# The tails' group: layer 1 by seven block products, PSUM tiles for each half of C, and last stores of two batches' rows each

## Chip, cores and metric

One core of a Trainium2 chip (trn2). The metric is device time in microseconds (us), the median of several executions; every execution also gives a span (from the first to the last instruction) and the clock that TensorE was granted. Some executions fall into a slower state, with a lower granted clock; times are compared between the others ("fast"), within the same rounds. By the rule of 2% a ratio within 2% of 1 counts as "same"; smaller differences are given with their interval.

## The reference

Eight batches of attention over a causal window of 64 positions, then a feed-forward block with layer norm and a residual:

```python
scores = q @ k.T / 8, masked to 0 <= i - j < 64;  attn = softmax(scores) @ v    # 8 heads, 576 positions, 64 wide
x = attn.transpose(0, 2, 1, 3).reshape(8, 576, 512)
xn = (x - mean) / sqrt(var + 1e-6) * g_ln
out = x + relu(xn @ w_ch1) @ w_ch2                                               # 512 -> 2048 -> 512
```

## The kernel before

It works in nine groups of 512 rows. Groups 0 to 7 hold the first 512 positions of one batch each; group 8, the tails' group, holds the last 64 positions of all eight batches: block kb (of four) has batch 2kb in partitions 0 to 63 and batch 2kb+1 in partitions 64 to 127. While TensorE does one group's feed-forward block, the other engines do the next group's attention, so in group 8 they have little to do.

Layer 1 is plain: 16 column blocks `hps`, each of four matmuls of 128x512. Layer 2 is a 2x2 block product done with seven products in place of eight; three banks A, B, C of PSUM (the memory in which TensorE accumulates) collect them, and VectorE adds each result to `xn` (the residual, which becomes the output) as soon as it stands:

```python
def product(n, p):                                   # p: which half (128 rows) of the product
    which, a, wv = {1: ("A", ...), 2: ("B", ...), 6: ("A", ...), 5: ("C", ...),
                    7: ("A", ...), 4: ("B", ...), 3: ("C", ...)}[n]       # cut
    ...
    for c in range(NHC // 2):                        # 8 matmuls of 128x256
        nc.tensor.matmul(out=bank[which][:, p, :], lhsT=a[:, c, 128*p:128*p+128], rhs=wv[:, c, :],
                         start=(first and p == 0 and c == 0), stop=(c == NHC//2 - 1), ...)

def stage(n, p):                                     # order of n: 1, 2, 6, 5, 7, 4, 3
    product(n, p)
    ...                                              # after the second half: post() adds a bank to xn
    elif n == 7: post("A", 2, 1); post("C", 2, 1); post("A", 2, 0)

def store_rest(k0, cols, eng):                       # the tails' rows of blocks k0 and k0+1
    xv = x_norm[(g, k0 // 2)]                        # [128 partitions, 2 blocks, 512]
    for r in range(2):                               # r: half of the partitions
        (eng or (nc.sync, nc.scalar)[r]).dma_start(
            out=out[2*k0+r : 2*k0+r+3 : 2, SM:S, cols].rearrange("k s d -> s k d"),   # [64 rows, 2 batches, cols]
            in_=xv[64*r : 64*r+64, :, cols])
```

The softmax here doesn't subtract the row's maximum and nothing guards it: scores larger than these inputs give would overflow.

## Time and profile before

| | kernel before |
|---|---|
| median (3 executions) | 313.59 us (313.27 to 313.82) |
| traced execution | 314.71 us, span 313.0 us, clock 0.999 |
| last group, layer 1 | 64 matmuls, 13.84 us |
| last group, layer 2 | 112 matmuls, 12.25 us |
| last matmul to the end of the span | 5.5 us |

```profile
SPq L838 <- DMA out_dram<-xn: 2.7, 1, 2.7
```

Look at the engines' sum first (TensorE is the bound), then at the wait for the last stores, 2.7 us. The chain of waits, the last instructions and the DMA shares of this kernel stand in the prediction.

### The profile page before, as it was taken

Reading aid. Unit: us, or ns where it says so; the run is one execution under the profiler, and the core shown is the slowest. Engines: PE = TensorE matmul, PEld = TensorE weight load, DVE = VectorE, ACT = ScalarE, POOL = GpSimd, SP = SyncE. Lnnn points to the kernel's source line nnn. Section 1 sums busy time; section 2 is a strip of 40 time slices with the busy share of each in tenths; the row PEclk is TensorE's granted clock in tenths of the full one; section 3 lists DMA queues with packets and bytes.
Section 4 is the critical chain, followed back from the end, with each engine's and each line's share of the span. In section 5 each row is a group of like instructions: output and inputs, shape, how many; then the busy total and the mean of one; then the engine's idle time right before and its main releaser. Section 6 shows DMA issues by size and latency. Waiting matters only on the chain.

```text
span 313.0 us, 7473 instructions
## 1 busy us (share of the span) xinstructions
PE 298.9 (95%) x3041; PEld 194.1 (62%) x3041; DVE 205.2 (66%) x385; ACT 153.4 (49%) x258; POOL 166.3 (53%) x251
## 2 busy tenths in 40 slices
PE   6988998899999999999999999999999999999992
PEld 4457544497554468646964686459646855784582
DVE  1689585855674996589666965896669636751642
ACT  1496633477416752776247526762475058306500
POOL 7578666454760798369814983698145506200000
PEclk9999999999999999999999999999999999999999
DMA  8999999998866996798179997993690393003013
GB/s 192 267 390 290 320 336 272 280 304 184 159 144 196 268 206 105 243 312 147 37 212 316 203 149 219 316 142 67 209 172 19 62 209 117 2 2 134 0 36 101
DMA packets 109892, 57.42 MB, mean 183 GB/s; under 512 B 79841, under 2 KB 100833, under 8 KB 109858
## 3 DMA queue, kind: packets, MB, share of 16 engines
q1 hardware_dynamic: 108944, 54.02, 69.1%
q0 software_dynamic: 768, 2.80, 3.7%
q8 instruction: 24, 0.39, 0.5%
q10 hardware_dynamic: 146, 0.13, 0.1%
q14 instruction: 10, 0.08, 0.1%
HBM read 38.80 MB, written 9.44 MB: 154 GB/s over the span
## 4 chain that ended last, share of the span: by engine, by line
PE 74%; DMA 10%; DVE 7%; SPq 4%; POOL 2%; ACT 1%; issue 1%; POOLq 0%; ACTq 0%
PE hps L392 30%; PE pA L464 11%; PE pC L464 7%; PE pB L464 7%; PE ch L404 6%; DMA w2s<-in_moe_w_ch_dram 4%; DMA qk<-in_k_dram 4%; PE xps L317 3%; PE sc L283 3%; PE hph L513 3%; PE tp L226 2%; SPq L141 2%; DVE sS L443 2%; DMA w1s<-in_moe_w_ch_dram 2%; SPq L89 1%; DVE pt L297 1%
## 5 line engine op out<-in xcount | busy, mean ns | idle before, releaser
L392 PE MATMUL hps<-zT,w1g 128*128 128x512 f16 x480 | 110.4, 379 | 0.0
L396 ACT ACTIVATE hrT<-hps 128x512 f16<-128x512 f32 x120 | 71.9, 599 | 50.7 <-PE hps L392 47.2
L392 PEld LDWEIGHTS <-w1g 128*128 128x128 f16 x480 | 44.6, 98 | 49.3 <-issue 1.0
L290 ACT ACTIVATE pt<-sc 128x512 f16<-128x512 f32 x72 | 39.0, 595 | 29.8 <-DVE xn L471 15.6
L464 PEld LDWEIGHTS <-sS 128*128 128x128 f16 x448 | 43.3, 98 | 5.1
L342 POOL TENSOR_SCALAR rsz<-mvg 128x1 f32<-128x1 f32 x28 | 10.7, 382 | 60.4 <-DVE mvg L328 59.8
L128 POOL CAST qk<-qk 128x1024 f16<-128x1024 f32 x32 | 35.1, 1112 | 13.4 <-DMA qk<-in_q_dram 6.9
L464 PEld LDWEIGHTS <-hrT 128*128 128x128 f16 x336 | 32.6, 98 | 5.2
L212 ACT COPY qkT<-tp 128x1024 f16<-128x1024 f16 x16 | 16.1, 1012 | 35.2 <-PE tp L226 26.1
L297 DVE TENSOR_TENSOR pt<-pt,mask 128x1024 f16<-128x1024 f16 x32 | 25.4, 800 | 11.9 <-ACT pt L290 11.9
L471 DVE TENSOR_TENSOR xn<-pA,xn 128x512 f32<-128x512 f32 x28 | 19.2, 686 | 21.1 <-PE pA L464 21.1
L443 DVE TENSOR_TENSOR sS<-hrT 128x512 f16<-128x512 f16 (+1 forms) x42 | 24.8, 591 | 10.2 <-ACT hrT L396 10.2
L464 PE MATMUL pA<-wT,sS 128*128 128x256 f16 x224 | 26.9, 273 | 0.0
L345 POOL TENSOR_SCALAR z<-xn,rsz 128x512 f16<-128x512 f32 x28 | 25.3, 902 | 2.9
L464 PE MATMUL pC<-w2s,sS 128*128 128x256 f16 x224 | 26.8, 273 | 0.0
L325 DVE BATCH_NORM_STATS2 stats<-xn 128x6 f32<-128x512 f32 x36 | 25.0, 695 | 1.2
L323 DVE TENSOR_TENSOR xn<-xps,rcp 128x512 f32<-128x512 f32 x36 | 24.9, 692 | 1.2
L513 PE MATMUL hph<-zT,w1g 128*128 128x256 f16 x192 | 23.2, 272 | 2.3 <-ACT zT L360 1.1
L320 DVE RECIPROCAL rcp<-xps 128x8 f32<-128x8 f32 x36 | 7.4, 205 | 26.8 <-PE xps L317 26.8
L404 PE MATMUL ch<-w2s,hrT 128*128 128x512 f16 x96 | 23.1, 380 | 0.0
L513 PEld LDWEIGHTS <-w1g 128*128 128x128 f16 x192 | 18.3, 98 | 5.1 <-issue 2.6
L317 PEld LDWEIGHTS <-pt 128*64 128x64 f16 x576 | 12.2, 110 | 14.4 <-issue 6.4
(85 smaller groups left out, 395.1 us busy)
## 6 DMA issues: line engine op xcount, KB each, us to landing
out_dram<-xn SPq DMA_DIRECT2D x34, 256.0 KB, 2.6
qk<-in_q_dram SPq DMA_DIRECT2D x16, 512.0 KB, 6.2
qk<-in_k_dram SPq DMA_DIRECT2D x16, 512.0 KB, 7.4
v<-in_v_dram SPq DMA_DIRECT2D x32, 256.0 KB, 6.5
w2s<-in_moe_w_ch_dram SPq DMA_DIRECT2D x12, 512.0 KB, 5.7
w1s<-in_moe_w_ch_dram SPq DMA_DIRECT2D x4, 512.0 KB, 6.7
tk<-in_k_dram SPq DMA_DIRECT2D x8, 256.0 KB, 4.7
tv<-in_v_dram SPq DMA_DIRECT2D x8, 256.0 KB, 5.3
```

Source lines behind the costliest of these rows:

```text
L128: nc.gpsimd.tensor_copy(out=dst[:, :].rearrange("p (a j) e d -> p a e j d", j=j), in_=t[:, :].rearrange("p (a e j d) -> p a e j d", e=2, j ...
L290: nc.scalar.activation(out=o, in_=i, func=AF.Exp, bias=0.0, scale=scale)
L297: nc.vector.tensor_tensor(out=ptv, in0=ptv, in1=mb, op=ALU.mult)
L323: nc.vector.tensor_tensor(out=xn, in0=xps[:, :, 0:D], in1=rcp_b, op=ALU.mult)
L325: nc.vector.bn_stats(out=stats, in_=xv)
L345: nc.gpsimd.tensor_scalar(out=z, in0=xv, scalar1=rs, scalar2=nm, op0=ALU.mult, op1=ALU.add)
L392: nc.tensor.matmul(out=hps, lhsT=w1g[:, kc, 128 * hc:128 * (hc + 1)], rhs=zT[g][:, kc, :], start=(kc == 0), stop=(kc == NKC - 1),)
L396: nc.scalar.activation(out=hrT[:, hc, :], in_=hps, func=AF.Relu, bias=0.0, scale=1.0)
L404: nc.tensor.matmul(out=ch[kb], lhsT=hrT[:, hc, 128 * kb:128 * (kb + 1)], rhs=w2s[:, hc, :], start=(hc == 0), stop=(hc == NHC - 1),)
L443: nc.vector.tensor_tensor(out=o, in0=x, in1=y, op=op)
L464: nc.tensor.matmul(out=bank[which][:, p, :], lhsT=a[:, c, 128 * p:128 * p + 128], rhs=wv[:, c, :], start=(first and p == 0 and c == 0), st ...
L513: nc.tensor.matmul(out=hps[:, e], lhsT=w1g[:, kc, 128 * hc:128 * (hc + 1)], rhs=zT[g][:, kc, 256 * half:256 * half + 256], start=(kc == 0) ...
```

## The change

Its intent: do layer 1 of the tails' group by seven block products as well, which needs 7/8 of TensorE's work; the sums it needs go to engines that idle there. And shorten the tail: two PSUM tiles for C, so that each half of the last product is added and stored on its own, stores of whole blocks (two batches' rows), all issued from SyncE but one. The core of the diff:

```diff
         def store_rest(k0, cols, eng):
             for r in range(2):
-                (eng or (nc.sync, nc.scalar)[r]).dma_start(
-                    out=out[2 * k0 + r:2 * k0 + r + 3:2, SM:S, cols].rearrange("k s d -> s k d"),
-                    in_=xv[64 * r:64 * r + 64, :, cols],
+                (nc.sync, eng)[r].dma_start(
+                    out=out[2 * (k0 + r):2 * (k0 + r) + 2, SM:S, cols],
+                    in_=xv[:, r, cols],
@@ product: C of the last group
+                    for r in range(2):
+                        bank[("C", r)] = ps_t.tile([128, 256], FP32, tag=f"t{r}", ...)
@@ stage
+            if last and n == 3:
+                post_c(0, p)
+                nc.sync.dma_start(out=out[2 * p:2 * p + 2, SM:S, 256:DM], in_=x_norm[(g, 0)][:, p, 256:DM])
+                return
             elif n == 7:
                 post("A", 2, 1)
-                post("C", 2, 1)
+                post_c(2, 0); post_c(2, 1)            # last group
                 post("A", 2, 0)
+                store_rest(2, slice(256, DM), nc.sync)
             elif n == 4:
-                    store_rest(2, slice(0, DM), nc.sync)
+                    store_rest(2, slice(0, 256), nc.gpsimd)
@@ new: layer 1 in four blocks d; A, B, C in PSUM
+        def l1_a(d):  product 1 -> A; ACT keeps A; product 2 -> B; DVE: B + kept, POOL: ReLU; product 5 -> C; ACT keeps C
+        def l1_b(d):  product 6 onto A; ACT keeps A; product 3 onto C; DVE: C + kept, ReLU
+        def l1_c(d):  product 7 onto A; DVE: A + kept C, ReLU
+        def l1_e(d):  product 4 onto A; ACT: ReLU
@@ last group's order
+                l1_b(0); for d in 1..3: l1_a(d); l1_c(d - 1); l1_b(d); l1_e(d - 1)
+                stage(1, 0); l1_c(3); stage(1, 1); l1_e(3); stage(2, ...); stage(5, ...); stage(6, ...)
+                for n in (7, 4, 3): ...
@@ group before: sums of W1 (4) and of z (4) on VectorE; l1_a(0) ahead of its product 3
```

(The four `l1_` functions are shortened to what they do.)

More of the change, by code (lines that the diff above doesn't have):

```diff
@@ L458, in product @@
             if p == 0 and n in (1, 2, 5):
-                if which == "C":
+                if which == "C" and last:
+                    for r in range(2):
+                        bank[("C", r)] = ps_t.tile([128, 256], FP32, tag=f"t{r}", name=f"pC{r}_{g}")
+                elif which == "C":
                     bank[which] = ps_t.tile([128, 2, 256], FP32, tag="t1", name=f"p{which}_{g}")
@@ L462, in product @@
                     bank[which] = ps_mm.tile([128, 2, 256], FP32, tag="mm", name=f"p{which}_{g}")
+            split_c = last and which == "C"
+            o = bank[(which, p)][:, :] if split_c else bank[which][:, p, :]
             for c in range(NHC // 2):
                 nc.tensor.matmul(
-                    out=bank[which][:, p, :], lhsT=a[:, c, 128 * p:128 * p + 128], rhs=wv[:, c, :],
-                    start=(first and p == 0 and c == 0), stop=(c == NHC // 2 - 1), skip_group_check=True,
+                    out=o, lhsT=a[:, c, 128 * p:128 * p + 128], rhs=wv[:, c, :],
+                    start=(first and (p == 0 or split_c) and c == 0), stop=(c == NHC // 2 - 1), skip_group_check=True,
                 )
@@ L471, in post, with post_c @@
             nc.vector.tensor_tensor(out=xv, in0=bank[which], in1=xv, op=ALU.add)
+        def post_c(kb0, r):
+            xv = x_norm[(g, kb0 // 2)][:, r, 256:512]
+            nc.vector.tensor_tensor(out=xv, in0=bank[("C", r)], in1=xv, op=ALU.add)
         last = g == NGRP - 1
@@ L476, in stage @@
             product(n, p)
+            if last and n == 3:
+                post_c(0, p)
+                nc.sync.dma_start(
+                    out=out[2 * p:2 * p + 2, SM:S, 256:DM],
+                    in_=x_norm[(g, 0)][:, p, 256:DM],
+                )
+                return
             if p == 0:
@@ L488, in stage @@
                 post("A", 2, 1)
-                post("C", 2, 1)
+                if last:
+                    post_c(2, 0)
+                    post_c(2, 1)
+                else:
+                    post("C", 2, 1)
                 post("A", 2, 0)
+                if last:
+                    store_rest(2, slice(256, DM), nc.sync)
             elif n == 4:
@@ L501, in stage @@
                 tbank["n"] = 0
-                if last:
-                    store_rest(0, slice(256, DM), None)
-                else:
-                    store(0)
-                    store(1)
+                store(0)
+                store(1)
         def l1_half(half, i):
@@ L533, in l2_two, with l1_product @@
                     add_out(kb)
+        lbank = {}
+        def l1_product(n, d):
+            w1v = w1g[:, :, :].rearrange("p (a k) (i e m) -> p a k i e m", a=2, e=2, m=128)
+            t1, t2, t3, t4 = (zS["sum"][:, m] for m in range(4))
+            z = zT[g]
+            which, a, b = {
+                1: ("A", w1v[:, 0, :, :, 0, :], z[:, 0:2, 0:256]),
+                2: ("B", w1v[:, 1, :, :, 0, :], z[:, 2:4, 0:256]),
+                5: ("C", w1S[1], t1),
+                6: ("A", w1S[2], t2),
+                3: ("C", w1S[4], z[:, 2:4, 256:512]),
+                7: ("A", w1S[3], t3),
+                4: ("A", w1v[:, 1, :, :, 1, :], t4),
+            }[n]
+            if n == 1:
+                pool, tag = (ps_mm, "mm") if d == 2 else (ps_s, "sc")
+                lbank[("A", d)] = pool.tile([128, 2, 256], FP32, tag=tag, name=f"lA_{d}")
+            elif n == 2:
+                lbank[("B", d)] = ps_t.tile([128, 2, 256], FP32, tag="t0", name=f"lB_{d}")
+            elif n == 5:
+                if d % 2:
+                    lbank[("C", d)] = ps_t.tile([128, 2, 256], FP32, tag="t1", name=f"lC_{d}")
+                else:
+                    lbank[("C", d)] = ps_x.tile([128, 4, 256], FP32, tag="xps", name=f"lC_{d}")[:, 0:2]
+            o = lbank[(which, d)]
+            for r in range(2):
+                for kc in range(2):
+                    nc.tensor.matmul(
+                        out=o[:, r, :], lhsT=a[:, kc, 2 * d + r, :], rhs=b[:, kc, :],
+                        start=(n in (1, 2, 5) and r == 0 and kc == 0), stop=(kc == 1), skip_group_check=True,
+                    )
@@ new lines, in l1_quad, with l1_part, l1_keep, l1_sum @@
+        def l1_quad(d, e, h):
+            return hv[:, 2 * d:2 * d + 2, e, 256 * h:256 * h + 256]
+        def l1_part(x, d):
+            return zS[x][:, d % 2, :].rearrange("p (r t) -> p r t", r=2)
+        def l1_keep(x, which, d):
+            nc.scalar.copy(out=l1_part(x, d), in_=lbank[(which, d)])
+        def l1_sum(o, which, x, d):
+            nc.vector.tensor_tensor(out=o, in0=lbank[(which, d)], in1=l1_part(x, d), op=ALU.add)
+            eng = nc.gpsimd if x == "s1" else nc.vector
+            eng.tensor_scalar(out=o, in0=o, scalar1=0.0, scalar2=None, op0=ALU.max)
@@ new lines, in l1_a, with l1_b, l1_c @@
+        def l1_a(d):
+            l1_product(1, d)
+            l1_keep("s1", "A", d)
+            l1_product(2, d)
+            l1_sum(l1_quad(d, 0, 0), "B", "s1", d)
+            l1_product(5, d)
+            l1_keep("s5", "C", d)
+        def l1_b(d):
+            l1_product(6, d)
+            l1_keep("u2", "A", d)
+            l1_product(3, d)
+            l1_sum(l1_quad(d, 0, 1), "C", "u2", d)
+        def l1_c(d):
+            l1_product(7, d)
+            l1_sum(l1_quad(d, 1, 1), "A", "s5", d)
@@ new lines, in l1_e, with plan @@
+        def l1_e(d):
+            l1_product(4, d)
+            nc.scalar.activation(out=l1_quad(d, 1, 0), in_=lbank[("A", d)], func=AF.Relu, bias=0.0, scale=1.0)
+        if last:
+            def plan():
+                yield
+                l1_b(0)
+                for d in range(1, 4):
+                    l1_a(d)
+                    l1_c(d - 1)
+                    l1_b(d)
+                    l1_e(d - 1)
+                s_sums(0, 4)
+                stage(1, 0)
+                l1_c(3)
+                s_sums(0, 4, 1)
+                s_sums(4, 8, 1)
+                stage(1, 1)
+                l1_e(3)
+                s_sums(0, 4, 2)
+                stage(2, 0)
+                s_sums(4, 8, 2)
+                stage(2, 1)
+                stage(5, 0)
+                s_sums(0, 4, 3)
+                stage(5, 1)
+                s_sums(4, 8, 3)
+                stage(6, 0)
+                stage(6, 1)
+                s_sums(0, 4, 4)
+                s_sums(4, 8, 4)
+                for n in (7, 4, 3):
+                    for p in range(2):
+                        stage(n, p)
+                yield
+            l1_a(0)
+            return plan(), s_sums
@@ L552, in mlp_units, with w1_sums, z_sums @@
         return units, s_sums
+    w1S = {}
+    def w1_sums(*which):
+        wv = w1g[:, :, :].rearrange("p (a k) (i e m) -> p a k i e m", a=2, e=2, m=128)
+        a11, a12, a21, a22 = (wv[:, b, :, :, a, :] for a, b in ((0, 0), (0, 1), (1, 0), (1, 1)))
+        for n in which:
+            w1S[n] = p_in.tile([128, NKC // 2, NHC // 2, 128], FP16, tag=f"qk32_{n % 2}", name=f"w1S{n}")
+            o = w1S[n][:, :, :, :]
+            x, y, op = {1: (a21, a22, ALU.add), 2: (w1S.get(1), a11, ALU.subtract),
+                        3: (a11, a21, ALU.subtract), 4: (a12, w1S.get(2), ALU.subtract)}[n]
+            nc.vector.tensor_tensor(out=o, in0=x, in1=y, op=op)
+    zS = {}
+    def z_sums(g, *which):
+        if not zS:
+            t = p_in.tile([128, 4, 512], FP32, tag="v32", name="zsums", bufs=1)
+            zS["s5"] = t[:, 2:4, :]
+            zS["s1"] = p_in.tile([128, 2, 512], FP32, tag="tk32", name="s1sums", bufs=1)
+            zS["u2"] = p_in.tile([128, 2, 512], FP32, tag="tv32", name="u2sums", bufs=1)
+            zS["sum"] = t[:, 0:2, :].rearrange("p a n -> p (a n)").bitcast(FP16).rearrange(
+                "p (n k t) -> p n k t", n=4, k=2)
+        b11, b12 = zT[g][:, 0:2, 0:256], zT[g][:, 0:2, 256:512]
+        b21, b22 = zT[g][:, 2:4, 0:256], zT[g][:, 2:4, 256:512]
+        t1, t2, t3, t4 = (zS["sum"][:, n] for n in range(4))
+        for n in which:
+            o, x, y = {1: (t1, b12, b11), 2: (t2, b22, t1), 3: (t3, b22, b12), 4: (t4, b21, t2)}[n]
+            nc.vector.tensor_tensor(out=o, in0=x, in1=y, op=ALU.subtract)
     def w2_sums(i, c0, c1):
@@ L662, with begin_last @@
     load_qk(2, 1)
+    def begin_last():
+        nonlocal rest
+        rest, _ = mlp_units(NGRP - 1)
+        next(rest)
+    rest = None
     TAILS = {3: [0], 5: [1], 7: [2, 3]}
     for g in range(NGRP):
+        if g == NGRP - 1:
+            for _ in rest:
+                pass
+            break
         units, s_sums = mlp_units(g, (8, 16)[g] if g < 2 else 0, g == 0, g > 1)
@@ L806 @@
             at(8, t_tail, TAILS[g][1], 1)
+        if g == NGRP - 2:
+            at(0, w1_sums, 1, 2)
+            at(3, w1_sums, 3)
+            at(21, w1_sums, 4)
+            at(24, z_sums, NGRP - 1, 1, 2)
+            at(25, z_sums, NGRP - 1, 3, 4)
+            at(27, begin_last)
         for i, u in enumerate(units):
```

## The prediction

> **What bounds the kernel now.** I read the page first (busy shares and its 40 slices), then the chain of waits from 281.2 us to the end, then the timeline of the last microseconds, then the DMA view. TensorE is busy for 95% of the span at full granted clock, so what counts is TensorE's own work plus whatever lies behind its last matmul. The change touches only the last group (the tails' rows of all eight batches) and, on VectorE alone, the group before it. The chain of waits of that stretch:
>
> ```profile
> 281.35 13.84 PE hps L392 x64
> 295.19 1.75 PE pA L464 x16
> 296.94 1.75 PE pB L464 x16
> 298.69 1.75 PE pA L464 x16
> 300.44 1.75 PE pC L464 x16
> 302.18 1.75 PE pA L464 x16
> 303.93 1.75 PE pB L464 x16
> 305.68 1.76 PE pC L464 x16
> 307.44 0.02 issue
> 307.46 0.69 DVE xn L471
> ```
>
> Columns: start, length, what. There is no gap: layer 1 is 64 matmuls of 512 columns at 13.84/64 = 0.216 us, layer 2 is seven products of 16 matmuls of 256 columns at 1.75/16 = 0.109 us. No wait costs anything here. After the last matmul comes one VectorE addition, then stores:
>
> ```profile
> 306.88 1.98 SPq L424 DMA_DIRECT2D out_dram<-xn  x3
> 307.04 0.38 PE L464 MATMUL pC<-w2s,sS 128*128 128x256 f16 x2
> 307.46 0.69 DVE L471 TENSOR_TENSOR xn<-pC,xn 128x512 f32<-128x512 f32 x1 [0.61 <-PE pC L464]
> 308.18 0.70 ACTq L424 DMA_DIRECT2D out_dram<-xn  x1
> ```
>
> The span ends at 313.0, so the tail behind the last matmul is 5.5 us. It is the DMA engines' throughput that fills it: stretches of the DMA's share (last two columns: mean share of 16 engines, GB/s):
>
> ```profile
> 282.50:284.30 1.80, 1.80 (x10) 0.82 (x9) 0.00 (x0) 1.29 (x3) 0.00 (x0) 1.00 1.03 385
> 300.80:302.10 1.30, 1.30 (x14) 1.17 (x13) 0.70 (x2) 0.00 (x0) 0.00 (x0) 1.00 0.89 191
> 308.40:311.40 3.00, 0.00 (x0) 0.00 (x0) 0.00 (x0) 0.00 (x0) 0.00 (x0) 1.00 0.93 241
> 311.50:313.00 1.50, 0.00 (x0) 0.00 (x0) 0.00 (x0) 0.00 (x0) 0.00 (x0) 0.76 0.00 0
> ```
>
> The four last stores (two of 256 KB, two of 128 KB) keep all 16 engines 93% busy from 308.4 to 311.4; 1.6 us later the program ends. Stores of 128 partitions (first line) ran at 385 GB/s, those of 64 partitions (second line) at 191.
>
> **What the Trainium skill says.** (1) "DMA: Bandwidth & Descriptors", section "Why a DMA increments its semaphore by 16 and not by 1": a DMA is split along the slowest dimension of both access patterns, over the largest number k of engines, at most 16, that divides both sizes; on the SyncE and ScalarE queues these are the lowest-numbered k. Its section "Rules for kernel authors" says that an outermost dimension below 16 confines the whole DMA to that many engines. Every large transfer of the kernel before has 64 or 128 outermost and the trace shows them on all engines, so no transfer of it contradicts or tests this. The trace also records the destination as written: the old tail stores are 64 rows outermost, 2 batches inside. (2) "TensorE: Matmul & The Clock Gate", section "Wait — 56ns, not 53.3ns?": N columns take N/2.4 GHz + 2.5 ns, 109 ns for 256 and 216 for 512. The trace has 109 and 216: smaller matmuls lose almost nothing. (3) "VectorE: DVE Perf Modes", section "The perf-mode tier table (the rule you actually need)": tensor_tensor runs at one element a cycle with PSUM or fp32 operands, at two for fp16 in SBUF. The trace agrees: 0.69 us for 512 fp32, 0.42 for 512 fp16, 0.69 for 1024 fp16.
>
> **Layer 1, TensorE.** The new form has 7 products x 4 blocks x 4 matmuls = 112 of 256 columns, 112 x 0.109 = 12.2 us in place of 13.84. Gain 1.6 us, all on the path, if nothing waits.
>
> **The added work beside it.** In the group before, VectorE gets four sums of W1 (2048 fp16 a partition; from 0.42 at 512 and 0.69 at 1024, an estimate of 1.22 us each) and four of z at 0.42: 6.6 us. They are put where VectorE is idle (2.6 us before the mask, 2.1 before a reciprocal, 2.5 before the post of product 7), so TensorE should not feel them. In layer 1, per block: ScalarE three copies and a ReLU, 4 x 0.60 = 2.4 us; VectorE three additions with PSUM and two ReLUs, 3 x 0.69 + 2 x about 0.3 = 2.7; POOL one ReLU, about 0.8. TensorE takes 28 x 0.109 = 3.06 a block. Each engine fits, but tightly, so latencies show:
> - An accumulator's reader starts 0.20 us after the matmul's slot ends (the last pC: 305.51 + 16 x 0.109 = 307.26, VectorE at 307.46); with 0.69 for the addition and an estimated 0.06 back to TensorE a turn-round is 0.95. Product 4 accumulates on what product 7 left, and only products 6 and 3 (8 x 0.109 = 0.87) lie between. Laid out in order, with VectorE still at the previous addition in two cases, it waits 0.1, 0.2, 0.2, 0.1.
> - Layer 2's second product needs the ReLU of the very last product 4: 0.2.
> - The order of layer 2 in this group becomes 1, 2, 5, 6, 7 where it was 1, 2, 6, 5, 7. The addition that reads bank A after product 6 now stands right in front of product 7, which accumulates on A; nothing covers its turn-round: 0.95.
>
> Sum 1.7, against 1.6 gained. So I expect the last matmul at about the old time, 307.4 us.
>
> **The end.** With two PSUM tiles the last addition is 128x256: 0.69 - 256/0.96 ns = 0.42 us, 0.27 less, so the last store can be issued at about 308.0 instead of 308.18. Four stores had been issued from 306.88 on, 768 KB; half of those bytes for rows 2 and 3 now go out after product 7, some 1.8 us earlier. If they ran on 16 engines the tail would be latency only: issue at 308.0, first packet 1.24 us later (the stores issued at 299.44 have theirs at 300.68), last about 0.5 later, 1.6 to the end: span 311.4, a gain of 1.6.
>
> But the new destination is two batches of 64 rows, outermost 2, against 128 partitions. By the rule above k is 2: each 128 KB store runs on engines 0 and 1 alone, 64 packets of 1 KB each. In the packet records such a packet takes 46 ns undisturbed (the commonest of 12,800) and packets of one engine do not overlap (2 KB in 84 ns is 24.4 GB/s, x16 = 390, what the first line shows). So 64 x 0.046 = 2.94 us a store, one behind the other on the same two engines:
> - two stores after product 2, issued 299.3: 300.5 to 306.4, hidden;
> - two after product 7 (columns 256 on), ready from 306.3: to 312.3;
> - one after product 4 (the other goes by GpSimd): to 315.2;
> - two after the halves of product 3: to 321.1.
>
> Plus 1.6 to the end: span 322.7, and with the 0.6 by which the untraced median exceeds the traced span (313.59 against 313.0): 323.3 us. If GpSimd's store falls on the same two engines, 2.9 more: 326.2.
>
> **Rivals.**
> A. *The stores spread over 16 engines after all* (the compiler reorders the destination, or splits it to match the 128 partitions). For: it is a natural way to write the store, and a tuner who times it would see the loss. Against: the trace shows the old destination's dimensions kept as written. Time: 313.6 + 0.1 - 1.6 = 312.1.
> B. *As A, and the turn-rounds cost nothing* (or the product order is no wait): 310.4, still within 2%.
> C. *As A, but VectorE becomes the bound*: about 21 us of its work now lies in 27 us, and one late addition shifts all behind it; the two-source additions with fp16 may also hold up POOL's ReLU, which layer 2 needs first. Against: 3.06 us a block hold 2.7. Time 313 to 315.
> D. *k is 2 but stores on different pairs of engines*: then each takes 2.9 us beside the others: 308.0 + 1.2 + 2.9 + 1.6 + 0.6 = 314.3. Against: the page says lowest-numbered.
>
> **Range and chances.** I give the confinement to two engines three chances in four; then the time is 321 to 326.5, as packets take 40 or 46 ns and as GpSimd's store shares the pair or not, over the limit of 319.9 in nearly all cases. The rest lies at 310.5 to 315, within 2% (the limit is 307.3; even B does not reach it). A range for 8 in 10 has to span both: 311.6 to 326.6. Point 323.3.
>
> **What would show it.** In the changed profile: (1) DMA share of about 0.12 (2/16) and some 45 GB/s over the last 10 us, long after the last matmul, with stores landing 6 us and more after issue; shares of 0.9 would be A. (2) Seven products of layer 1 at 0.44 us, TensorE's last matmul between 306.5 and 308.5. (3) A TensorE gap of about 0.9 us ahead of product 7 in layer 2, released by VectorE's addition. (4) Small waits ahead of product 4 in layer 1, released by VectorE. (5) The last addition at 0.42 us. (6) The group before unchanged, its TensorE without new gaps. I am wrong if stores land in 2 to 3 us: then the answer is about 312.

## More of the kernel before

The page's first part and its list of transfers (engine, operation, number, KB each, us from issue to landing), with SyncE's own wait at the very end (us in total, times, longest):

```profile
span 313.0 us, 7473 instructions
...
PE 298.9 (95%) x3041; PEld 194.1 (62%) x3041; DVE 205.2 (66%) x385; ACT 153.4 (49%) x258; POOL 166.3 (53%) x251
...
out_dram<-xn SPq DMA_DIRECT2D x34, 256.0 KB, 2.6
```

## The result and the profile after

| | before | after |
|---|---|---|
| median of the same rounds | 313.43 us | 326.59 us (325.90 to 328.23, 4 executions) |
| traced execution | 314.71 us, span 313.0 | 327.09 us, span 325.1 |
| VectorE starts the last addition | 307.46 | 307.19 |
| last packet of the stores ends | 311.5 | 323.5 |

The ratio of the two is 1.0432 (95% interval 1.0384 to 1.0480). Ratios here are the mean time of one kernel's fast executions over that of the other's of the same rounds, so not quite the ratio of the medians quoted.

The first part of the page after. TensorE is busy a little less than before and the span is 12 us longer, so the time is not in work:

```profile
span 325.1 us, 7628 instructions
...
PE 297.6 (92%) x3089; PEld 198.2 (61%) x3089; DVE 217.4 (67%) x411; ACT 153.2 (47%) x258; POOL 172.8 (53%) x256
```

The last instructions of the kernel after (start, length, engine, what; in brackets the engine's idle time before it and who ended it):

```profile
299.06 1.91 PE L469 MATMUL pA<-wT,sS 128*128 128x256 f16 x16
301.00 0.69 DVE L476 TENSOR_TENSOR xn<-pA,xn 128x512 f32<-128x512 f32 x1 [1.00 <-PE pA L469]
...
301.75 1.91 PE L469 MATMUL pA<-wT,sS 128*128 128x256 f16 x16 [0.78 <-DVE xn L476]
...
306.87 0.92 POOL L424 DMA_DIRECT2D out_dram<-xn  x1 [13.75 <-DVE xn L476]
307.19 0.42 DVE L480 TENSOR_TENSOR xn<-pC,xn 128x256 f32<-128x256 f32 x1 [0.29 <-PE pC L469]
307.21 8.62 SPq L488 DMA_DIRECT2D out_dram<-xn  x2
```

The first three lines are products 6 and 7 and the addition between them: the wait foretold. The last addition takes 0.42 in place of 0.69 us and starts 0.27 us earlier. At 307.6 all arithmetic is done, where the kernel before had 308.15; yet the program ends at 325.1. Stretches of the DMA of the kernel after (last two columns: mean share of 16 engines, GB/s), against 0.93 and 241 before:

```profile
301.00:303.50 2.50, 1.75 (x17) 1.56 (x17) 1.89 (x3) 0.00 (x0) 0.00 (x0) 1.00 0.13 40
...
309.40:312.50 3.10, 0.00 (x0) 0.00 (x0) 0.00 (x0) 0.00 (x0) 0.00 (x0) 0.55 0.19 50
312.50:316.40 3.90, 0.00 (x0) 0.00 (x0) 0.00 (x0) 0.00 (x0) 0.00 (x0) 0.50 0.13 48
316.40:323.50 7.10, 0.00 (x0) 0.00 (x0) 0.00 (x0) 0.00 (x0) 0.00 (x0) 0.50 0.13 47
323.50:325.10 1.60, 0.00 (x0) 0.00 (x0) 0.00 (x0) 0.00 (x0) 0.00 (x0) 0.50 0.00 0
```

A share of 0.13 is two engines of sixteen. The stores run on for 15.9 us after the last addition (307.61 to 323.51); the 0.19 in one stretch comes with 16-byte packets on GpSimd's queue. Three more views: GpSimd's store by its time to landing (9.9 us), SyncE's wait for the stores at the end, and the two last issues of SyncE, whose durations (min/median/max in ns) are thousands of ns where the issues of the kernel before's tail take 595 to 702:

```profile
out_dram<-xn POOLq DMA_DIRECT2D x1, 128.0 KB, 9.9
```
```profile
SPq L1007 <- DMA out_dram<-xn: 7.9, 2, 5.2
```
```profile
L488 SPq DMA_DIRECT2D out_dram<-xn x2: 3613/4260/4907, 307.2 to 310.9; - x2
```

The chain of waits is no help at this end: from 293.1 to 306.8 it has nothing but "issue", and it ends with GpSimd's wait (POOLq L1007), not with SyncE's last stores. Where the chain does that, go to the DMA's shares.

The trace's packet records give each store of SyncE's queue (128 packets of 1 KB, median 46 ns each), in order:

| store | first packet to last | length |
|---|---|---|
| after product 2, block 0 | 300.11 to 303.53 | 3.4 |
| after product 2, block 1 | 303.52 to 306.25 | 2.7 |
| after product 7, block 2 | 306.24 to 309.73 | 3.5 |
| after product 7, block 3 | 309.69 to 312.53 | 2.8 |
| after product 4, block 2 | 312.53 to 317.86 | 5.3 |
| product 3, first half | 317.82 to 320.58 | 2.8 |
| product 3, second half | 320.54 to 323.51 | 3.0 |

They stand one behind the other. The records carry no engine number; that it is two engines follows from the share and from 64 x 0.046 = 2.94 us a store. Completion also shows the number of engines: the seven stores end with 14 semaphore writes on SyncE's queue, two each; in the kernel before every tail store has 16. GpSimd's store (32 packets of 4 KB at 159 ns: 16 x 0.159 = 2.54 us on each of two engines) runs from 312.28 to 316.33, beside the fifth store, which takes 2.5 us more than its neighbours. The share stays at 0.13 while both are under way: both are on the same two engines.

### The profile page after: what moved, and what is told of

Same layout as the page of the kernel before. It is cut to its first block, busy times and chain, and to the rows that moved or that the text cites. A ratio compares the mean times of both kernels' runs of the same rounds, so it can differ in the third digit from the quotient of the medians.

```text
span 325.1 us, 7628 instructions
## 1 busy us (share of the span) xinstructions
PE 297.6 (92%) x3089; PEld 198.2 (61%) x3089; DVE 217.4 (67%) x411; ACT 153.2 (47%) x258; POOL 172.8 (53%) x256
## 4 chain that ended last, share of the span: by engine, by line
PE 62%; DMA 14%; DVE 5%; SPq 5%; issue 5%; POOL 3%; POOLq 0%; ACT 0%
PE hps L392 24%; PE pA L469 9%; PE pC L469 6%; PE pB L469 6%; PE ch L404 5%; DMA w2s<-in_moe_w_ch_dram 4%; DMA qk<-in_k_dram 4%; SPq L141 4%; PE xps L317 3%; PE sc L283 3%; DMA vB<-vA 3%; DMA w1s<-in_moe_w_ch_dram 2%; DVE sS L443 2%; PE tp L226 1%; PE lA L582 1%
## 5 line engine op out<-in xcount | busy, mean ns | idle before, releaser
L392 PE MATMUL hps<-zT,w1g 128*128 128x512 f16 x416 | 96.3, 380 | 0.0
L396 ACT ACTIVATE hrT<-hps 128x512 f16<-128x512 f32 x104 | 62.3, 599 | 38.6 <-PE hps L392 35.1
L392 PEld LDWEIGHTS <-w1g 128*128 128x128 f16 x416 | 38.3, 98 | 42.0 <-issue 0.9
L532 PEld LDWEIGHTS <-w1g 128*128 128x128 f16 x192 | 18.0, 98 | 5.8 <-issue 2.0
```

What stands on the lines that cost most here:

```text
L392: nc.tensor.matmul(out=hps, lhsT=w1g[:, kc, 128 * hc:128 * (hc + 1)], rhs=zT[g][:, kc, :], start=(kc == 0), stop=(kc == NKC - 1),)
L396: nc.scalar.activation(out=hrT[:, hc, :], in_=hps, func=AF.Relu, bias=0.0, scale=1.0)
L532: nc.tensor.matmul(out=hps[:, e], lhsT=w1g[:, kc, 128 * hc:128 * (hc + 1)], rhs=zT[g][:, kc, 256 * half:256 * half + 256], start=(kc == 0) ...
```

## The experiments

Theory P: a destination with 2 outermost confines a store to two DMA engines, and eight such stores stand in line. Rival Q: it is SyncE's one queue with nearly all stores in it. Rival L: layer 1 and the waits it brings are the loss. Eleven runs of nine kernels; all gave correct results. The rounds ran on different chips, and the kernel before differs by 0.9 us between them, so go by the ratios. By the rule of 2% e2 and e4 are slower and all others the same.

| run | what | median us (before, same rounds) | ratio, 95% interval |
|---|---|---|---|
| e1_rows64 | after, 64 rows outermost | 313.20 (314.59) | 0.997, 0.994 to 1.000 |
| e2_before_pairs | before, new destinations | 327.33 (314.59) | 1.0422, 1.0385 to 1.0459 |
| e3_l1_only | before, new layer 1 and order | 313.49 (314.59) | 0.9971, 0.9947 to 0.9995 |
| e4_pool16 | after, only GpSimd's store on 16 engines | 324.21 (314.59) | 1.0311, 1.0287 to 1.0334 |
| e8_one_pair | e1, only the last store in the new form | 316.43 (313.69) | 1.0086, 1.0052 to 1.0119 |
| e5_order | e1, order 1, 2, 5, 6, 3, 7, 4 | 311.58 (313.69) | 0.9943, 0.9911 to 0.9976 |
| e6_order_2q | e5, halves on two queues | 311.47 (313.69) | 0.9917, 0.9890 to 0.9943 |
| e7_rows64_2q | e1, halves on two queues | 312.76 (313.69) | 0.9966, 0.9941 to 0.9991 |
| f1_l1_again | e3 again | 313.48 (314.22) | 0.9984, 0.9949 to 1.0019 |
| f2_before_tail | before, only the tail's halves and stores | 313.05 (314.22) | 0.9967, 0.9934 to 0.9999 |
| f3_best_again | e6 again | 312.20 (314.22) | 0.9937, 0.9906 to 0.9968 |

**e1_rows64.** Undo one part of the change.

```diff
-                    out=out[2 * (k0 + r):2 * (k0 + r) + 2, SM:S, cols],
-                    in_=xv[:, r, cols],
+                    out=out[2 * k0 + r:2 * k0 + r + 3:2, SM:S, cols].rearrange("k s d -> s k d"),
+                    in_=xv[64 * r:64 * r + 64, :, cols],
@@ product 3
-                nc.sync.dma_start(out=out[2*p:2*p+2, SM:S, 256:DM], in_=x_norm[(g, 0)][:, p, 256:DM])
+                for b in range(2):
+                    (nc.sync, nc.scalar)[b].dma_start(
+                        out=out[2*p+b, SM:S, 256:DM], in_=x_norm[(g, 0)][64*b:64*b+64, p, 256:DM])
```

> The changed kernel, with only the destinations of the tails' stores turned back: 64 rows outermost, two batches inside (store_rest), and for the two halves of product 3 one store per batch of 64 rows (SyncE and ScalarE). Queues otherwise as in the change. Theory P (a destination with 2 outermost confines each store to two DMA engines): the stores spread over 16 engines again, the DMA share in the last 5 us is 0.5 to 0.9, stores land in 2 to 4 us, span 310.9, time 311.5 to 312.5, 1.5 to 2 us below the kernel before. Rival Q (it is the one SyncE queue that holds nearly all stores, not the engines): the queue is as long as before, so 320 us or more. Rival L (layer 1 and the waits it brings are the loss): 324 us or more, since none of that is touched.

The loss is gone, with as many stores on SyncE's queue. DMA stretches of this run:

```profile
299.00:300.20 1.20, 0.58 (x6) 0.38 (x4) 0.58 (x1) 0.00 (x0) 0.00 (x0) 1.00 0.85 181
305.10:309.10 4.00, 0.67 (x7) 0.35 (x4) 0.84 (x3) 0.00 (x0) 0.71 (x1) 1.00 0.80 195
309.10:310.70 1.60, 0.00 (x0) 0.00 (x0) 0.00 (x0) 0.00 (x0) 0.00 (x0) 0.52 0.00 0
```

Shares of 0.8 and a span of 310.7: Q and L fall. The time missed the band of 311.5 to 312.5 by 0.7 us, but so did the kernel before in these rounds (314.59 where 313.6 was assumed); the difference of 1.4 us is just under the foretold 1.5 to 2.

**e2_before_pairs.** One part alone: the kernel before with the new `out=` and `in_=` of `store_rest`, nothing else.

> The kernel before, with only the destinations of its six tail stores in the new form (two batches outermost, 128 partitions); its queues, its layer 1 and its order stay. Theory P: 64 packets of 1 KB on each of two engines take 64 x 0.046 = 2.94 us a store, of 2 KB 64 x 0.084 = 5.4 us; two short ones hide behind TensorE, two long and two short ones stand after 308.1: 308.1 + 16.7 + 1.6 = 326.4 us of span, about 327 us. Rival Q: the last store stays on ScalarE's queue and the issue count is the old one, so 313 to 314. Rival L: nothing of layer 1 is changed, 313.5.

327.33 against the 327 worked out from two packet times. The new form of the tails' stores alone makes the whole loss, without any of layer 1, and with the last store on ScalarE's queue. The edit changes the source too, from 64 to 128 partitions; no run parts the two, but the stores of whole groups read 128 partitions and ran on all engines (share 1.03, first of the prediction's DMA stretches), so a 128-partition source alone doesn't confine a store. ScalarE's packets lie within those of SyncE's (312.06 to 319.74 of 307.07 to 324.23), and the share stays at that of two engines, so another issuing engine gives no other pair:

```profile
312.00:320.00 8.00, 0.00 (x0) 0.00 (x0) 0.00 (x0) 0.00 (x0) 0.00 (x0) 0.50 0.13 50
```

**e3_l1_only and f1_l1_again.** The change with the old C bank, the old last addition and the old stores; twice, since the first one's traced execution (319.83 us, clock 0.988) is left out.

> The change's layer 1 by seven products and its order of layer 2, with the old bank for C (one tile, one addition at the end) and the old stores. Theory P: the net of gain and waits alone; in the changed kernel's trace the last matmul's slot ends at 306.99 against 307.26 before, so 0.2 to 0.4 us faster than before: 313.0 to 313.4. Rival L: 320 us or more. Rival Q: as theory P.

> The same kernel as e3_l1_only (layer 1 by seven products and its product order alone, old bank for C, old stores), again, because the traced execution of that run was in the slow state and its three timed ones gave only an interval of 0.2 to 1.7 us. By the slow trace the stretch from the last product 4 of the group before to the last matmul is 27.65 us against 27.83 in the kernel before: 0.2 us faster, ratio 0.998 to 1.000. If layer 1 is worth the 1.6 us that its matmuls save: 0.995.

Layer 1 by seven products is worth 0.2% (interval from -0.5 to +0.2%) in the second run and 0.3% in the first: a small gain or none. The chain of waits of f1 shows where the 1.6 us of saved matmuls went:

```profile
292.73 0.44 PE lA L569 x4
293.17 0.87 PE pA L466 x8
294.04 0.50 PE lA L569 x4
294.54 0.66 PE pB L466 x6
...
295.23 1.27 PE pB L466 x10
296.50 1.75 PE pC L466 x16
298.25 1.76 PE pA L466 x16
...
300.03 0.70 DVE xn L473
...
300.77 1.91 PE pA L466 x16
```

From product 6's end (300.01) to product 7's (302.68) pass 2.67 us in place of 1.75: 0.92 lost to the addition's turn-round. Product 2 takes 1.96 (0.21 lost, waiting for the last ReLU), product 4's four blocks some 0.05 to 0.08 each, 0.2 in all. Sum 1.4 of 1.6; the stretch from the group before's last product 4 to the last addition is 27.67 us against 27.85 before.

**e4_pool16.** Only GpSimd's store, as two of one batch each.

```diff
-                    store_rest(2, slice(0, 256), nc.gpsimd)
+                    nc.sync.dma_start(out=out[4:6, SM:S, 0:256], in_=x_norm[(g, 1)][:, 0, 0:256])
+                    for b in range(2):
+                        nc.gpsimd.dma_start(out=out[6+b, SM:S, 0:256], in_=x_norm[(g, 1)][64*b:64*b+64, 1, 0:256])
```

> The changed kernel, with only GpSimd's one store made into two stores of one batch each (64 rows outermost), still from GpSimd; the seven on SyncE stay in the new form. Theory P with GpSimd's store on the same two engines: in the changed trace the fifth store of SyncE takes 5.3 us where its neighbours take 2.8; with GpSimd's bytes on all 16 engines it takes 2.8 to 3.2, so 2 to 2.5 us faster than the change: 324.1 to 324.6. If GpSimd's store had run on a pair of its own (my prediction's point): within 0.4 us of the change, 326.2 to 327.0.

324.21, inside the first band. SyncE's fifth store now takes 3.0 us (311.87 to 314.85) in place of 5.3, and from the end of the last addition to the last packet it is 13.4 us in place of 15.9. So GpSimd's store did run on the same two engines and cost about 2.5 us (2.4 by the medians; 3.8 by the ratios, since the kernel before was 1.2 us slower in these rounds than in the change's own).

**e8_one_pair.** One dose: e1 with only the very last store in the new form.

> As e1_rows64 (64 rows outermost everywhere), but the very last store, the second half of product 3, alone in the change's form with two batches outermost: one dose of the suspected cost where the change has eight. Theory P: 64 packets on each of two engines, 2.94 us, in place of two stores of 0.4 to 0.8 us on 16 engines: span 2.2 to 2.7 us over e1_rows64, about 315.5 us if the kernel before takes 314.6 (ratio to before 1.002 to 1.006). If the cost needs a queue of such stores (rival Q), nothing: ratio 0.997.

3.6 us over e1 by the ratios (3.7 over e7 below, of the same rounds), more than foretold. In the traces the last packet ends 6.1 us after the last addition, in e1 2.9. Its DMA stretches:

```profile
308.00:311.00 3.00, 0.00 (x0) 0.00 (x0) 0.00 (x0) 0.00 (x0) 0.00 (x0) 1.00 0.64 151
311.00:314.00 3.00, 0.00 (x0) 0.00 (x0) 0.00 (x0) 0.00 (x0) 0.00 (x0) 0.63 0.11 36
```

The last store's 64 packets on each engine need 2.94 us, but until 311.3 other stores' packets are under way too, on all engines and so on these two; I had counted only the difference of two undisturbed stores. One such store costs as much as it has packets on an engine, plus what it must share; no row of them is needed.

**e5_order, e6_order_2q, e7_rows64_2q.** Can the change be made to pay? e5 puts product 3 between 6 and 7, so the addition of A after product 6 has a product to hide behind; C's two additions need only product 5 and move up to it; product 4, now last, gets the halves. Shortened:

```diff
-                stage(5, *); s_sums(3); stage(6, *); s_sums(4);  then n in (7, 4, 3)
+                stage(5, 0); post_c(2, 0); s_sums(0, 4, 4); stage(5, 1); post_c(2, 1); s_sums(4, 8, 4)
+                stage(6, 0); s_sums(0, 4, 3); stage(6, 1); s_sums(4, 8, 3);  then n in (3, 7, 4)
@@ product 4 of the last group: PSUM tiles ("B", 0), ("B", 1); each half added and stored (one store per batch)
```

> As e1_rows64, with layer 2 of the tails' group in the order 1, 2, 5, 6, 3, 7, 4: the additions for C after product 5 at once, product 3 between 6 and 7, so that the addition that reads bank A after product 6 has 1.75 us to hide in; product 4 is last, with a PSUM tile and a store for each half. Theory: the wait of 0.8 us ahead of product 7 goes, the last matmul comes 0.7 to 0.8 us earlier, and 256 KB fewer stand in line at the end: 0.8 to 1.5 us under e1_rows64, ratio to before 0.992 to 0.995. Rival: VectorE, which now has to give the sums for product 3 earlier and five results in the last 2 us, makes a new wait of the same length: ratio 0.997 as e1_rows64.

> As e5_order, with the two 64-partition halves of every tail store on two queues, SyncE and ScalarE, so that they are issued at the same time. Theory: with 128 partitions read at once a packet takes 46 instead of some 76 ns and the second issue (0.6 us) does not wait: 0.2 to 0.6 us under e5_order. Rival: the queues interleave on the same engines, nothing is won: as e5_order within 0.2.

> As e1_rows64, with the two halves of every tail store on SyncE and ScalarE, and none on GpSimd. Same theory and rival as in e6_order_2q, on the change's own order: 0.2 to 0.6 us under e1_rows64 (ratio to before 0.995 to 0.996), or no difference.

The order does what was foretold: 0.9943 is inside its band. By the times alone that is not clear (the interval overlaps that of e7, of the same rounds), but the stretch from the group before's last product 4 to the last addition is 26.73 us in e5 and 27.68 in e1, and the chain of e6 has no VectorE between products 6, 3 and 7:

```profile
297.17 1.75 PE pA L472 x16
298.92 1.75 PE pC L472 x16
300.66 1.76 PE pA L472 x16
```

The two queues are not shown to help: e7 equals e1 (0.9966 and 0.997), and e6's interval overlaps e5's. In e6 ScalarE's packets took 46 ns (median), SyncE's still 74. The rival holds there, as far as these runs can tell.

**f2_before_tail and f3_best_again.** What of the best version's gain is due to the stores, what to layer 1?

> The kernel before with its layer 1 and its order 1, 2, 6, 5, 7, 4, 3, but C in two PSUM tiles for the tails' group, the last addition in two halves with a store for each batch, columns 256 on of rows 2 and 3 stored after product 7, and the two halves of each store on SyncE and ScalarE. The tail after the last matmul was 5.5 us; in e7_rows64_2q, with the same stores, it is 4.9 us. So 0.5 to 0.7 us under the kernel before, ratio 0.998. Rival: the tail's gain needs layer 1's (then 1.000), or the stores are worth more than that (0.995).

> The same kernel as e6_order_2q (seven products in layer 1, order 1, 2, 5, 6, 3, 7, 4, halves of the last product, two queues), on the same chip and rounds as the two above: ratio 0.990 to 0.994. What remains after the ratios of the two others are taken off is the order, 0.8 us by the wait ahead of product 7.

The tail alone gives 0.3% (0.9967), the whole 0.6% (0.9937; 0.8% in its first run). Both intervals are wide and overlap; the traces say it more sharply: the stretch to the last addition is 26.7 us in e6, 27.67 in the change and 27.85 before. e6_order_2q is the fastest version found, 0.6 to 0.8% under the kernel before, though not shown to be apart from e5.

## Why the prediction came out as it did

- **Two engines a store: right.** Rule, packet time (46 ns), 2.94 us a store, the line of stores behind one another: e1 and e2 show it from both sides, and the packet records show the line.
- **The step that failed: which engines GpSimd's store uses.** The prediction's sum let the fifth store end at 315.2, with "the other goes by GpSimd" costing nothing; the other case ("If GpSimd's store falls on the same two engines, 2.9 more: 326.2") was named, without a chance of its own, and left out of the point. It fell on the same pair: the fifth store ended at 317.86, and e4 puts the cost at about 2.5 us. With it the foretold span of 322.7 becomes 325.2; the measured one is 325.1. The top of the range, 326.6, left only 0.4 us above that case.
- **A smaller mis-size in the same sum, 0.9 of the miss of 3.3 us:** the conversion from span to time. I took 0.6 us from a median of 313.59 and a span of 313.0 that belong to different executions. Within one execution the time is 1.7 to 2.0 us over the span (314.71 and 313.0 before, 327.09 and 325.1 after), and the traced execution of the kernel before happened to be 1.1 us slower than its median, that of the kernel after only 0.5.
- **Luck in the span:** stores began with some packets slower than 46 ns (3.4 and 3.5 us for the first of each pair), partly made up by an earlier start (300.1, foretold 300.5). A reading was off, without weight: by the packet records the stores issued at 299.44 in the kernel before have their first packet at 300.75, not 300.68, so 1.31 us after the issue and not 1.24.
- **Layer 1: mechanism and size right.** Foretold 1.7 us of waits against 1.6 saved; measured 1.4 against 1.6. The turn-round between 6 and 7 was 0.92 (0.95 foretold), ahead of product 2 0.21 (0.2), product 4 0.2 in all where 0.6 was foretold. GpSimd's ReLU took 1.49 us against an estimated 0.8; no matmul waited for it.
- **The last addition: right,** 0.42 us. **The group before:** TensorE has no new gap there; VectorE's busy time rises by some 5 us and stays out of the way.
- **Rivals A to D:** A (16 engines after all) is refuted by the shares of 0.13, and e1, which makes it true, shows it would have been a gain of 0.3%. B falls with A, and by the 0.92 us between products 6 and 7. D (different pairs) falls by the packet records. C did not appear: VectorE was busy for 22.3 of the 27.7 us, but is never what TensorE waits for except in the turn-rounds.

## What to carry to other kernels

Write the DRAM side of a store so that its outermost dimension is a long one (the 64 rows here); a leading dimension of 2, harmless to look at, makes a 128 KB store an affair of two engines and 3 us, and several such stores stand in line whatever queue issues them. When an engine's work is cut, look at the turn-rounds of accumulators first: here seven products saved 1.6 us and the waits took back 1.4, until e5 and e6 put another product between the one that writes a bank and the next that accumulates on it, so that the addition had time to read the bank.

## What the Trainium skill lacked or had wrong

- "DMA: Bandwidth & Descriptors", section "Why a DMA increments its semaphore by 16 and not by 1": the rule for k, the number of engines, held exactly (two semaphore writes for each of SyncE's seven stores, 16 for GpSimd's, as the section has it for a queue of its kind). It leaves open where GpSimd's cursor stands: here its only store with 2 outermost came to the pair that SyncE's stores use (a share of 0.13 with both under way; 2.5 us, e4), after twelve GpSimd transfers of 64 partitions.
- The same page says nothing of an issue that itself lasts long: SyncE's last two issues took 3.6 and 4.9 us while earlier stores were unfinished (3.1 and 2.8 in e4), its others 0.5 to 0.7. In e2 an issue behind unfinished stores took 0.5, so what makes it long is not shown.
- "GPSIMD Engine Reference", section "4.1 Engine selection", calls one-input work on GpSimd roughly line-rate. A maximum with 0 on 512 fp16 in place took 1.49 us there (four of them) and 0.29 on VectorE (eight); GpSimd's scaling of 512 fp32 to fp16 took 0.77 us in the group before. No page gives the first figure. VectorE was busy for 11.1 of the 14 us from 282 to 296; whether that slows GpSimd was not tested:

```profile
L599 DVE TENSOR_SCALAR hrT<-hrT x8: 294/294/295, 284.4 to 294.9; 128x512 f16<-128x512 f16 x8
L599 POOL TENSOR_SCALAR hrT<-hrT x4: 1486/1486/1497, 281.8 to 291.6; 128x512 f16<-128x512 f16 x4
```
